# Keys and values as head pairs without tails, states on four 64x64 tiles, and the query cast that moved with them

## The chip, the cores and the metric

One core of one Trainium2 chip. The metric is the device time of one execution in microseconds (us). Engines: PE multiplies matrices, ACT, DVE and POOL (GpSimd) work on vectors, SP issues transfers. Words used below: a "turn" of queries or rows is their transposition on PE, by matmuls with the identity ("the turn to batch 1" is the passage from one batch to the next); the "stream" is the run of a batch's feed-forward matmuls on PE; a "burst" is the matmuls of one batch's state product; the "chain" is the profile's view of the work that ended last, followed back through what each piece waited for.

## The reference, cut to what matters

```python
kv  = einsum('bhsd,bhse->bhde', k, v)      # a 64x64 state for each of 8 heads, 576 rows; 8 batches
out = einsum('bhsd,bhde->bhse', q, kv)
out = out / sqrt(mean(out*out, -1) + 1e-6) * g_norm
x   = out as 4608 rows of 512
xn  = x / sqrt(mean(x*x, -1) + 1e-6) * rms_g
result = (silu(xn @ w_gate) * (xn @ w_val)) @ w_out      # 512 -> 1536 -> 512
```

The feed-forward part is nearly all of the work. The kernel runs it in nine passes (batches 0 to 7 with 512 rows each, then the eight tails of 64 rows as a ninth) and computes the attention of pass n+1 while pass n streams through PE.

## The kernel before

The state product of batches 2 to 7 takes the rows in five chunks of 128; the last chunk holds only the tail's 64 rows, the rest is zero. Batches 0 and 1 (`EARLY`) already have head pairs over 128 partitions.

```python
def kv_pair(ps, b, j, first, last):
    if b < EARLY:                       # 9 chunks, rows 0:64 are one head, 64:128 the other
        for c in range(C):
            for u in range(2):
                rows = slice(u * D, u * D + D)
                PE.matmul(ps[rows, rows], lhsT=pairs_buf(b, "k")[rows, j, c, :], rhs=pairs_buf(b, "v")[rows, j, c, :], ...)
        return
    for t in range(T + 1):              # 5 chunks of 128 rows, one column half for each head
        for u in range(2):
            cols = slice(u * D, u * D + D)
            PE.matmul(ps[cols, cols], lhsT=bufs[b]["k"][:, t, 2 * j + u, :], rhs=bufs[b]["v"][:, t, 2 * j + u, :], ...)

# ... the turn from batch 0 to batch 1 (cut)
att1.kv_products()
for i, engine in enumerate((DVE, SC, DVE, SC)):
    cast_q(1, slice(2 * i, 2 * i + 2), engine)
att1.kv_copy()
# ...
alloc_q(2)
for i in range(2):
    cast_q(2, slice(4 * i, 4 * i + 4), GP)      # batch 2's queries, on POOL
down_part(0, 2, 4)
turns.q_turn(0, SC)                             # first turn of batch 1's queries
# ... F.sums, F.head, F.root: a chain of short DVE instructions, F1y is its last
xs = [F.scale(c, F.outa[c]) for c in range(4)]  # four scalings on DVE, xna
ffn.down_out(0)                                 # output copy on ACT
down_part(1, 8, 12)
f_x(0, xs[0], SC)                               # turn the scaled rows on PE, copy on ACT
f_x(1, xs[1], SC)
ffn.down_out(1)
down_part(2, 8, 12)
f_x(2, xs[2], DVE)                              # needs the bank that f_x(0)'s copy frees
f_x(3, xs[3], DVE)
```

## Time and profile before

| | before |
|---|---|
| time, median of 3 (range) | 320.73 us (320.5 to 321.9) |
| PE busy in a steady batch of 32.7 us | all of it |
| PE idle in the turn from batch 0 to 1 | 0.9 us |
| state product of a steady batch on the chain | 0.75 us |

How to read it: as long as PE has no gap, only matmul time counts. All else counts only in the first 56 us, where PE waits for transfers and then for DVE's short chain, and at one wait near 95 us.

### The profile page before, as it was taken

How to read it: one execution, taken by the hardware profiler on the slowest of the kernel's cores; microseconds unless marked ns; L12 is line 12 of the kernel's file. 1: busy time of each engine (PE TensorE's matmuls, PEld its weight loads, DVE VectorE, ACT ScalarE, POOL GpSimd, SP SyncE). 2: the span in 40 equal slices, each digit the busy share in tenths (PEclk: the TensorE clock that was granted, in tenths of full speed). 3: DMA queues.
4: the chain of work that ended last, by engine and by line, in shares of the span. 5: the costliest groups of instructions: out<-in, count | busy, mean ns of one | idle time of the engine just before them, and what ended most of it. 6: DMA issues, size and time to landing. Idle time of an engine off the chain costs nothing.

```text
span 319.5 us, 5632 instructions
## 1 busy us (share of the span) xinstructions
PE 311.2 (97%) x2179; PEld 151.1 (47%) x2179; DVE 182.2 (57%) x371; ACT 176.1 (55%) x312; POOL 24.8 (8%) x50
## 2 busy tenths in 40 slices
PE   8799998999999999999999999999999999999994
PEld 3485455444444444444444444444444444444443
DVE  4686758679438922893279417951795079504310
ACT  3587456375667466737683767376744374233321
POOL 1274354200000000000000000000000000000000
PEclk9999999999999999999999999999999999999998
DMA  7999999899389657924791389946002600330014
GB/s 263 362 385 387 376 374 293 164 253 241 67 159 312 159 136 189 315 55 113 193 337 48 82 180 229 316 86 197 2 2 60 190 14 1 63 137 0 0 36 99
DMA packets 72903, 54.90 MB, mean 172 GB/s; under 512 B 42280, under 2 KB 64044, under 8 KB 72876
## 3 DMA queue, kind: packets, MB, share of 16 engines
q1 hardware_dynamic: 72496, 53.88, 59.8%
q10 hardware_dynamic: 380, 0.66, 0.6%
q8 instruction: 17, 0.28, 0.4%
q14 instruction: 10, 0.08, 0.1%
HBM read 37.75 MB, written 9.44 MB: 148 GB/s over the span
## 4 chain that ended last, share of the span: by engine, by line
PE 89%; DMA 4%; DVE 2%; SPq 2%; ACT 1%; issue 0%; DVEq 0%
PE g_ps L501 28%; PE v_ps L501 27%; PE o_ps L543 25%; DMA st<-in_v_dram 2%; SPq L319 2%; DMA st<-in_k_dram 1%; PE att_ps L278 1%; PE v_ps L518 1%; PE g_ps L518 1%; DMA qt<-qb 1%; PE att_ps L270 1%; PE g_ps L543 1%; PE v_ps L543 1%; DMA out_dram<-o_sb 1%; DVE xna L482 1%; PE o_ps L518 1%
## 5 line engine op out<-in xcount | busy, mean ns | idle before, releaser
L507 DVE TENSOR_TENSOR h_sb<-silu,v_ps 128x512 bf16<-128x512 bf16 x104 | 71.1, 684 | 98.9 <-ACT silu L506 67.8
L501 PE MATMUL g_ps<-xnt,wg_sb 128*128 128x512 bf16 x416 | 106.9, 379 | 0.0
L501 PE MATMUL v_ps<-xnt,wv_sb 128*128 128x512 bf16 x416 | 106.8, 379 | 0.0
L506 ACT ACTIVATE silu<-g_ps 128x512 bf16<-128x512 f32 x104 | 62.0, 596 | 72.2 <-PE g_ps L501 56.8
L543 PE MATMUL o_ps<-wo_sb,h_sb 128*128 128x512 bf16 x396 | 87.8, 379 | 0.0
L501 PEld LDWEIGHTS <-wv_sb 128*128 128x128 bf16 x416 | 40.7, 98 | 49.1
L543 PEld LDWEIGHTS <-h_sb 128*128 128x128 bf16 x420 | 40.6, 98 | 47.7 <-issue 0.4
L501 PEld LDWEIGHTS <-wg_sb 128*128 128x128 bf16 x416 | 39.6, 98 | 46.4
L106 ACT COPY o_sb<-o_ps 128x512 f32<-128x512 f32 (+1 forms) x34 | 19.7, 579 | 38.1 <-PE o_ps L543 37.3
L106 ACT CAST vb<-st 128x512 bf16<-128x512 f32 (+2 forms) x30 | 17.2, 628 | 4.2 <-DMA st<-in_v_dram 4.2
L397 DVE TENSOR_TENSOR xna<-outa,s1y 128x512 bf16<-128x512 bf16 x28 | 17.9, 683 | 0.0
L380 DVE TENSOR_REDUCE ssq<-sqt 128x16 f32<-128x1024 bf16 x14 | 17.1, 1220 | 0.5
L380 DVE TENSOR_REDUCE ssq<-sq 128x16 f32<-128x1024 bf16 x14 | 17.1, 1219 | 0.5
L106 ACT CAST qb<-st 128x1024 bf16<-128x1024 f32 (+1 forms) x16 | 14.4, 935 | 1.9 <-DMA st<-in_q_dram 1.9
L106 ACT CAST kb<-st 128x512 bf16<-128x512 f32 (+1 forms) x25 | 14.0, 619 | 0.0
L366 ACT ACTIVATE sq<-att_ps 128x512 bf16<-128x512 f32 x14 | 7.6, 594 | 4.3 <-PE att_ps L357 3.6
L643 PE MATMUL att_ps<-kv_all 128*128 128x512 bf16 (+1 forms) x23 | 8.4, 491 | 1.2 <-DVE sel L632 1.2
L379 DVE TENSOR_TENSOR sq<-sq,gsq 128x512 bf16<-128x512 bf16 x14 | 5.9, 422 | 4.9 <-ACT sq L366 4.9
L108 POOL CAST wo_sb<-st 128x512 bf16<-128x512 f32 x12 | 7.3, 633 | 7.4 <-DMA st<-in_moe_w_out_dram 7.4
L108 DVE CAST kb<-st 128x576 bf16<-128x576 f32 (+1 forms) x12 | 5.9, 512 | 3.0 <-DMA st<-in_k_dram 2.9
L366 ACT ACTIVATE sqt<-o_ps 128x512 bf16<-128x512 f32 x14 | 7.6, 598 | 0.0
L371 ACT CAST outa<-att_ps 128x512 bf16<-128x512 f32 x14 | 7.5, 593 | 0.0
(148 smaller groups left out, 185.9 us busy)
## 6 DMA issues: line engine op xcount, KB each, us to landing
out_dram<-o_sb SPq DMA_DIRECT2D x14, 512.0 KB, 3.0
st<-in_q_dram SPq DMA_DIRECT2D x6, 1024.0 KB, 6.5
st<-in_k_dram SPq DMA_DIRECT2D x6, 1024.0 KB, 11.4
st<-in_v_dram SPq DMA_DIRECT2D x6, 1024.0 KB, 12.0
st<-in_moe_w_out_dram SPq DMA_DIRECT2D x6, 512.0 KB, 10.4
st<-in_moe_w_gate_dram SPq DMA_DIRECT2D x4, 512.0 KB, 9.7
st<-in_moe_w_val_dram SPq DMA_DIRECT2D x4, 512.0 KB, 9.2
st<-in_k_dram SPq DMA_DIRECT2D x4, 288.0 KB, 4.3
```

The source lines that it names most:

```text
L106: engine.copy(out=dst, in_=src)
L108: engine.tensor_copy(out=dst, in_=src)
L366: SC.activation(out=self.sq[i][:, :, 0, g:H:2, :], in_=self.banks[i][g], func=ACT.Square)
L371: SC.copy(out=rows[:, :, g:H:2, :], in_=self.banks[i][g])
L380: DVE.reduce_sum(out=self.ssq[:, c], in_=sq, axis=AX.X)
L397: DVE.tensor_tensor(out=self.xna[c], in0=self.outa[c], in1=self.alpha[:, c, :].to_broadcast([128, H, D]), op=OP.mult)
L501: PE.matmul(ps, lhsT=wt[:, s, j * 128 : (j + 1) * 128], rhs=x[:, s, :], start=(s == 0), stop=(s == NS - 1),)
L506: SC.activation(out=silu, in_=g_ps, func=ACT.Silu)
L507: DVE.tensor_tensor(out=self.h[:, j, :], in0=silu, in1=v_ps, op=OP.mult)
L518: PE.matmul(ps[:, u, lo % 256 : lo % 256 + hi - lo], lhsT=wt[:, s, j * 128 : (j + 1) * 128], rhs=xnts[self.n][:, s, lo:hi], start=(s == 0) ...
L543: PE.matmul(self.o_ps[c], lhsT=self.h[:, j, c * 128 : (c + 1) * 128], rhs=wo_sb[:, j, :], start=(j == 0), stop=(j == NF - 1),)
L643: PE.matmul(ps[:, 0:w], lhsT=warm_sb[:, 0:128], rhs=warm_sb[:, 0:w], start=True, stop=True, skip_group_check=True)
```

## The change

Its intent: load every batch's keys and values as pairs of heads over 128 partitions (one transfer of 2304-byte runs instead of a main part and a tail), so that no chunk is half empty, and run the state product on all four 64x64 tiles: even pairs on the two straight tiles, odd pairs on the two crossed ones. The states of odd pairs then lie crossed, and queries, outputs and squares follow. In passing it moves batch 2's query cast from POOL to ACT and DVE, and its state product one unit earlier. The core of the diff:

```diff
-EARLY = 2
 def load_kv(b, name, queue, js=slice(0, NS)):
-    src = srcs[name][b]
-    if b < EARLY: ...                                # paired view
-    queue.dma_start(out=main part, ...)              # 1024-byte runs
-    queue.dma_start(out=tail, ...)                   # 256-byte runs
+    view = srcs[name][b].rearrange("h s d -> (h s d)").rearrange("(j p x) -> p j x", j=NS, p=128)
+    queue.dma_start(out=raws[b, name][:, js, :], in_=view[:, js, :])
 def kv_products(self):
-    self.kv_ps = att_pool.tile([128, NS, 128], FP32, name="att_ps")
-    for j in range(NS):
-        kv_pair(self.kv_ps[:, j, :], self.n, j, j == 0, j == NS - 1)
+    self.kv_ps = [att_pool.tile([128, 2, D], FP32, name="att_ps") for _ in range(2)]
+    for a in range(2):
+        for c in range(C):
+            for x in range(2):
+                for g in range(2):
+                    rows, to = slice(g * D, g * D + D), slice((g ^ x) * D, (g ^ x) * D + D)
+                    PE.matmul(self.kv_ps[x][to, a, :], lhsT=kb[rows, 2 * a + x, c, :], rhs=vb[rows, 2 * a + x, c, :], ...)
 def kv_copy(self):
-    SC.copy(out=kv_all[0:D, n, :, 0:D], in_=ps[0:D, :, 0:D])
-    DVE.tensor_copy(out=kv_all[D:128, n, :, D:128], in_=ps[D:128, :, D:128])
+    for x, engine in enumerate((SC, DVE)):
+        for g in range(2):
+            rows, cols = slice(g * D, g * D + D), slice((g ^ x) * D, (g ^ x) * D + D)
+            cast(engine, kv_all[rows, self.n, x::2, cols], self.kv_ps[x][rows])
 # ... output products, squares, heads: crossed indices, same counts (cut)
-DVE.memset(kv_all[:, 0 : B - 1], 0.0)
+DVE.memset(kv_all[:, 0:2], 0.0)
 # the turn to batch 1
-for i, engine in enumerate((DVE, SC, DVE, SC)):
-    cast_q(1, slice(2 * i, 2 * i + 2), engine)
+for h in (0, 4):
+    cast_heads(1, h, 2, 1, DVE)
+    cast_heads(1, h + 2, 1, 1, SC)
+    cast_heads(1, h + 3, 1, 1, DVE)
 att1.kv_copy()
-alloc_q(2)
-for i in range(2):
-    cast_q(2, slice(4 * i, 4 * i + 4), GP)
 # ...
 ffn.down_out(0)
+alloc_q(2)
+for i in range(T):
+    cast_q(2, i, SC if i < 2 else DVE)
+# ... first two turns of batch 2's queries by transfer (cut)
 down_part(1, 8, 12)
 f_x(0, xs[0], SC)
 # later batches: 4 query casts of 2 heads, 4 + 4 key and value casts; batch 0's odd states crossed by two transfers (cut)
```

More of the change, by code (lines that the diff above doesn't have):

```diff
@@ L90 @@
     kv_all = consts.tile([128, B, NS, 128], BF16, name="kv_all")
-    kbs = [consts.tile([128, T + 1, H, D], BF16, name=f"kb{i}") for i in range(2)]
-    vbs = [consts.tile([128, T + 1, H, D], BF16, name=f"vb{i}") for i in range(2)]
+    kbs = [consts.tile([128, NS, C, D], BF16, name=f"kb{i}") for i in range(2)]
+    vbs = [consts.tile([128, NS, C, D], BF16, name=f"vb{i}") for i in range(2)]
     wg_sb = consts.tile([128, NS, d_ff], BF16, name="wg_sb")
@@ L101, in stage @@
     def stage(n=2048):
-        return stage_pool.tile([128, MAIN * T + MAIN], FP32, name="st")[:, 0:n]
+        return stage_pool.tile([128, NS * C * D], FP32, name="st")[:, 0:n]
     def cast(engine, dst, src):
@@ L116, in alloc_kv, with cast_kv, place @@
     def alloc_kv(b, name):
-        raws[b, name] = stage(MAIN * T + MAIN)
-    def pairs_raw(b, name):
-        return raws[b, name][:, 0 : NS * C * D].rearrange("p (j x) -> p j x", j=NS)
-    def pairs_buf(b, name):
-        flat = bufs[b][name].rearrange("p t h d -> p (t h d)")
-        return flat[:, 0 : NS * C * D].rearrange("p (j c d) -> p j c d", j=NS, c=C)
-    def load_kv(b, name, queue, js=slice(0, NS)):
-        src = srcs[name][b]
-        if b < EARLY:
-            view = src.rearrange("h s d -> (h s d)").rearrange("(j p x) -> p j x", j=NS, p=128)
-            queue.dma_start(out=pairs_raw(b, name)[:, js, :], in_=view[:, js, :])
-            return
-        raw = raws[b, name]
-        queue.dma_start(
-            out=raw[:, 0 : MAIN * T].rearrange("p (h x) -> p h x", h=H),
-            in_=src[:, 0:MAIN, :].rearrange("h (p t) d -> p h (t d)", t=T),
-        )
-        queue.dma_start(
-            out=raw[0:TAIL, MAIN * T :].rearrange("r (h d) -> r h d", h=H),
-            in_=src[:, MAIN:S, :].rearrange("h r d -> r h d"),
-        )
-    KV_CASTS = range(NS + 1)
-    def cast_kv(b, name, i, engine):
-        if b < EARLY:
-            cast(engine, pairs_buf(b, name)[:, i].rearrange("p c d -> p (c d)"), pairs_raw(b, name)[:, i, :])
-        elif i < NS:
-            hs = slice(2 * i, 2 * i + 2)
-            src = raws[b, name][:, 0 : MAIN * T].rearrange("p (h t d) -> p t h d", h=H, t=T)
-            cast(engine, bufs[b][name][:, 0:T, hs, :], src[:, :, hs, :])
-        else:
-            src = raws[b, name][0:TAIL, MAIN * T :].rearrange("r (h d) -> r h d", h=H)
-            cast(engine, bufs[b][name][0:TAIL, T], src)
+        raws[b, name] = stage(NS * C * D).rearrange("p (j x) -> p j x", j=NS)
+    def load_kv(b, name, queue, js=slice(0, NS)):
+        view = srcs[name][b].rearrange("h s d -> (h s d)").rearrange("(j p x) -> p j x", j=NS, p=128)
+        queue.dma_start(out=raws[b, name][:, js, :], in_=view[:, js, :])
+    def cast_kv(b, name, j, engine):
+        cast(engine, bufs[b][name][:, j].rearrange("p c d -> p (c d)"), raws[b, name][:, j, :])
+    def place(h):
+        return h if h % 4 < 2 else h ^ 1
     def load_q(b):
@@ L158, in load_q @@
         raws[b, "q"] = st
-        for hs in (slice(0, 4), slice(4, 8)) if b < EARLY else (slice(0, H),):
+        for hs in (slice(0, 4), slice(4, 8)) if b == 1 else (slice(0, H),):
             nc.sync.dma_start(
@@ L166, in alloc_q, with cast_heads, cast_q @@
         bufs[b]["q"] = qb_pool.tile([128, T, H, D], BF16, name="qb")
-    def cast_q(b, hs, engine):
-        src = raws[b, "q"].rearrange("p (h t d) -> p t h d", h=H, t=T)[:, :, hs, :]
-        cast(engine, bufs[b]["q"][:, :, hs, :], src)
+    def cast_heads(b, h, n, step, engine):
+        src = raws[b, "q"].rearrange("p (h t d) -> p t h d", h=H, t=T)
+        at = place(h)
+        cast(
+            engine, bufs[b]["q"][:, :, at : at + (n - 1) * step + 1 : step, :],
+            src[:, :, h : h + (n - 1) * step + 1 : step, :],
+        )
+    def cast_q(b, i, engine):
+        cast_heads(b, i, 2, 4, engine)
     def load_batch(b):
@@ L263, in alloc_xnt, with kv_pair @@
         xnts[n] = xnt_pool.tile([128, NS, MAIN], BF16, name="xnt")
-    def kv_pair(ps, b, j, first, last):
-        if b < EARLY:
-            for c in range(C):
-                for u in range(2):
-                    rows = slice(u * D, u * D + D)
-                    PE.matmul(
-                        ps[rows, rows], lhsT=pairs_buf(b, "k")[rows, j, c, :], rhs=pairs_buf(b, "v")[rows, j, c, :],
-                        start=(first and c == 0), stop=(last and c == C - 1),
-                    )
-            return
-        for t in range(T + 1):
+    def kv_pair(ps, j):
+        for c in range(C):
             for u in range(2):
-                cols = slice(u * D, u * D + D)
+                rows = slice(u * D, u * D + D)
                 PE.matmul(
-                    ps[cols, cols], lhsT=bufs[b]["k"][:, t, 2 * j + u, :], rhs=bufs[b]["v"][:, t, 2 * j + u, :],
-                    start=(first and t == 0), stop=(last and t == T),
-                )
-    def clear_tail_rows(i, engine):
-        for t in (kbs[i], vbs[i]):
-            engine.memset(t[TAIL:128, T], 0.0)
+                    ps[rows, rows], lhsT=kbs[0][rows, j, c, :], rhs=vbs[0][rows, j, c, :],
+                    start=(c == 0), stop=(c == C - 1),
+                )
     def to_rows(x, n, c, ps, engine):
@@ L306, in kv_products @@
         def kv_products(self):
-            self.kv_ps = att_pool.tile([128, NS, 128], FP32, name="att_ps")
-            for j in range(NS):
-                kv_pair(self.kv_ps[:, j, :], self.n, j, j == 0, j == NS - 1)
+            self.kv_ps = [att_pool.tile([128, 2, D], FP32, name="att_ps") for _ in range(2)]
+            kb, vb = bufs[self.n]["k"], bufs[self.n]["v"]
+            for a in range(2):
+                for c in range(C):
+                    for x in range(2):
+                        for g in range(2):
+                            rows, to = slice(g * D, g * D + D), slice((g ^ x) * D, (g ^ x) * D + D)
+                            PE.matmul(
+                                self.kv_ps[x][to, a, :], lhsT=kb[rows, 2 * a + x, c, :], rhs=vb[rows, 2 * a + x, c, :],
+                                start=(a == 0 and c == 0), stop=(a == 1 and c == C - 1),
+                            )
         def kv_copy(self):
-            n, ps = self.n, self.kv_ps
-            SC.copy(out=kv_all[0:D, n, :, 0:D], in_=ps[0:D, :, 0:D])
-            DVE.tensor_copy(out=kv_all[D:128, n, :, D:128], in_=ps[D:128, :, D:128])
+            for x, engine in enumerate((SC, DVE)):
+                for g in range(2):
+                    rows, cols = slice(g * D, g * D + D), slice((g ^ x) * D, (g ^ x) * D + D)
+                    cast(engine, kv_all[rows, self.n, x::2, cols], self.kv_ps[x][rows])
         def q_rows(self, c):
@@ L322, in q_rows @@
             )
-        def q_turn(self, pair, engine):
-            if pair == 0:
-                self.qt = qt_pool.tile([128, NS, MAIN], BF16, name="qt")
-            ps = att_pool.tile([128, NS, 2, 128], BF16, name="att_ps")
-            for i in range(2):
-                for j in range(NS):
-                    PE.matmul(
-                        ps[:, j, i, :], lhsT=bufs[self.n]["q"][:, 2 * pair + i, 2 * j : 2 * j + 2, :],
-                        rhs=identity, is_transpose=True,
-                        start=(i == 0 and j == 0), stop=(i == 1 and j == NS - 1),
-                    )
-            cast(engine, self.qt[:, :, 256 * pair : 256 * pair + 256], ps.rearrange("p j i t -> p j (i t)"))
         def o_products(self):
@@ L346, in o_products @@
                         rows = slice(g * D, g * D + D)
+                        cols = slice((g ^ j % 2) * D, (g ^ j % 2) * D + D)
                         ps = self.banks[c // 2][g][:, c % 2, j, :]
@@ L352, in o_products @@
                                 PE.matmul(
-                                    ps[us], lhsT=tails_q["t"][rows, c, j, us], rhs=kv_all[rows, 2 * c + u, j, rows],
+                                    ps[us], lhsT=tails_q["t"][rows, c, j, us], rhs=kv_all[rows, 2 * c + u, j, cols],
                                     **flags,
@@ L357, in o_products, with in_place @@
                             PE.matmul(
-                                ps, lhsT=self.qt[rows, j, 128 * c : 128 * c + 128], rhs=kv_all[rows, self.n, j, rows],
+                                ps, lhsT=self.qt[rows, j, 128 * c : 128 * c + 128], rhs=kv_all[rows, self.n, j, cols],
                                 **flags,
                             )
+        def in_place(self, rows, g):
+            fours = rows.rearrange("p c (a h) d -> p (c a) h d", h=4)
+            return fours[:, :, g : 4 - g : 3 - 2 * g, :]
         def put_squares(self, i):
@@ L365, in put_squares @@
             for g in range(2):
-                SC.activation(out=self.sq[i][:, :, 0, g:H:2, :], in_=self.banks[i][g], func=ACT.Square)
+                bank = self.banks[i][g].rearrange("p c (a b) d -> p (c a) b d", b=2)
+                SC.activation(out=self.in_place(self.sq[i][:, 0], g), in_=bank, func=ACT.Square)
         def put_rows(self, i):
@@ L370, in put_rows @@
             for g in range(2):
-                SC.copy(out=rows[:, :, g:H:2, :], in_=self.banks[i][g])
+                bank = self.banks[i][g].rearrange("p c (a b) d -> p (c a) b d", b=2)
+                SC.copy(out=self.in_place(rows, g), in_=bank)
             for c in range(2):
@@ L377, in sums @@
                 self.ssq = stat_pool.tile([128, T, 2, H], FP32, name="ssq")
-            sq = self.sq[c // 2][:, c % 2]
+            sq = self.sq[c // 2][:, :, c % 2]
             DVE.tensor_tensor(out=sq[:, 1], in0=sq[:, 0], in1=gsq8, op=OP.mult)
@@ L430, in turned_tiles @@
                 for g in range(2):
-                    rows = slice(g * D, g * D + D)
+                    rows, cols = slice(g * D, g * D + D), slice((g ^ u) * D, (g ^ u) * D + D)
                     PE.matmul(
-                        banks[g][out], lhsT=kv_all[rows, self.n, 2 * i + u, rows], rhs=self.qt[rows, 2 * i + u, :],
+                        banks[g][out], lhsT=kv_all[rows, self.n, 2 * i + u, cols], rhs=self.qt[rows, 2 * i + u, :],
                         start=True, stop=True,
@@ L678, in state0 @@
         warm(ps, max(dummies, 1), 512 if dummies else 128)
-        kv_pair(ps[:, 0:128], 0, j, True, True)
+        kv_pair(ps[:, 0:128], j)
         return ps
@@ L873 @@
                 round_w(4, "v", s, DVE)
-        if j == 7:
-            clear_tail_rows(0, DVE)
         if j == 8:
@@ L903, in f_heads @@
     def f_heads(j):
-        h = 4 * (j // 2) + j % 2
-        return slice(h, h + 3, 2)
+        h = 4 * (j // 2)
+        return slice(h + 1, h + 3) if j % 2 else slice(h, h + 4, 3)
     def f_o(c):
@@ L925 @@
     att1.kv_products()
-    for i, engine in enumerate((DVE, SC, DVE, SC)):
-        cast_q(1, slice(2 * i, 2 * i + 2), engine)
+    for h in (0, 4):
+        cast_heads(1, h, 2, 1, DVE)
+        cast_heads(1, h + 2, 1, 1, SC)
+        cast_heads(1, h + 3, 1, 1, DVE)
     att1.kv_copy()
-    clear_tail_rows(1, DVE)
     for blk in (1, 2):
@@ L932 @@
             round_wo(blk, i, 1, GP)
-    alloc_q(2)
-    for i in range(2):
-        cast_q(2, slice(4 * i, 4 * i + 4), GP)
     down_part(0, 2, 4)
@@ L961 @@
     ffn.down_out(0)
+    alloc_q(2)
+    for i in range(T):
+        cast_q(2, i, SC if i < 2 else DVE)
+    atts = {b: Att(b) for b in range(2, B + 1)}
+    for c in range(2):
+        atts[2].q_rows(c)
     down_part(1, 8, 12)
@@ L969 @@
     down_part(3, 8, 12)
-    atts = {b: Att(b) for b in range(2, B + 1)}
-    for c in range(T):
+    for c in range(2, 4):
         atts[2].q_rows(c)
@@ L987, in load_q_tails, with cast_q_tails, cross_states @@
         tails_q["b"] = qb_pool.tile([128, T, H, D], BF16, name="qb").rearrange("p t h d -> p t (h d)")
-    def cast_q_tails(c, n, engine):
-        cast(engine, tails_q["b"][:, c : c + n], tails_q["raw"][:, c : c + n])
+    def cast_q_tails(i, engine):
+        dst, src = (tails_q[nm].rearrange("p c (h d) -> p c h d", h=H) for nm in ("b", "raw"))
+        cast(engine, dst[:, :, place(i) : H : 4, :], src[:, :, i:H:4, :])
+    def cross_states():
+        for g in range(2):
+            rows, to = slice(g * D, g * D + D), slice((1 - g) * D, (1 - g) * D + D)
+            nc.sync.dma_start(out=kv_all[to, 0, 1::2, rows], in_=kv_all[rows, 0, 1::2, rows])
     def turn_q_tails(c):
@@ L1007 @@
             steps[0] += [lambda i=i: cast_kv(2, "k", i, DVE) for i in (2, 3)]
-            steps[0] += [lambda: cast_kv(2, "k", NS, GP)]
-            steps[0] += [lambda i=i: cast_kv(2, "v", i, GP) for i in (0, 1, NS)]
-            steps[2] += [lambda i=i: cast_kv(2, "v", i, DVE) for i in (2, 3)]
+            steps[0] += [lambda i=i: cast_kv(2, "v", i, GP) for i in (0, 1)]
+            steps[1] += [lambda i=i: cast_kv(2, "v", i, DVE) for i in (2, 3)]
+        if n == 3:
+            steps[3] += [cross_states]
         if n < B:
             a = atts[n + 1]
-            kv0 = 1 + 2 * int(n == 1)
+            kv0, o0 = (2, 4) if n == 1 else (1, 2)
             if not a.tail:
                 steps[kv0] += [a.kv_products, a.kv_copy]
-            steps[kv0 + 1] += [a.o_products]
+            steps[o0] += [a.o_products]
             for i in range(2):
-                u = kv0 + 1 + 2 * i
+                u = o0 + 2 * i
                 steps[u] += [lambda a=a, i=i: a.put_squares(i)]
@@ L1030 @@
             steps[10] += [lambda b=b: alloc_q(b)]
-            for i in range(2):
-                steps[11] += [lambda b=b, i=i: cast_q(b, slice(4 * i, 4 * i + 4), SC)]
-            for i in KV_CASTS:
-                steps[12 + i // 3] += [lambda b=b, i=i: cast_kv(b, "k", i, SC)]
-                steps[14 + i // 3] += [lambda b=b, i=i: cast_kv(b, "v", i, SC)]
+            for i in range(T):
+                steps[11] += [lambda b=b, i=i: cast_q(b, i, SC)]
+            for i in range(NS):
+                steps[12 + i // 2] += [lambda b=b, i=i: cast_kv(b, "k", i, SC)]
+                steps[14 + i // 2] += [lambda b=b, i=i: cast_kv(b, "v", i, SC)]
             for c in range(T):
@@ L1038 @@
         if b == B:
-            for i in range(2):
-                steps[11] += [lambda i=i: cast_q_tails(2 * i, 2, SC)]
+            for i in range(T):
+                steps[11] += [lambda i=i: cast_q_tails(i, SC)]
             for c in range(T):
```

## The prediction

> **What bounds the kernel now.** I read the page first (engine shares and the chain that ended last), then busy time by stretch, then the chain in order of time around one batch, around the last batch and around batch 1, and then the timeline where the chain leaves TensorE.
>
> ```profile
> span 319.5 us, 5632 instructions
> PE 311.2 (97%) x2179; PEld 151.1 (47%) x2179; DVE 182.2 (57%) x371; ACT 176.1 (55%) x312; POOL 24.8 (8%) x50
> 39.40:56.20 16.80, 15.93 (x198) 9.01 (x197) 12.07 (x28) 10.31 (x18) 8.08 (x13) 1.00 1.08 332
> 154.30:187.00 32.70, 32.70 (x218) 15.24 (x217) 19.09 (x37) 20.81 (x37) 0.00 (x0) 1.00 0.65 169
> ```
>
> Busy PE need not mean a bound PE, but from 56 to 312 us the chain confirms it: it is matmuls end to end. In the fourth line PE is busy for the whole 32.7 us of a batch, ACT for 20.8. In the third (the turn from batch 0 to batch 1) PE idles 0.9 us. So a change pays only by (a) taking matmul time out of the steady batches, or (b) shortening the stretches before 56 us where PE waits. A shorter DMA, a saved cast, a free DVE microsecond buys nothing elsewhere.
>
> The chain at a steady batch's attention part, at the tail batch's, and at batch 1's:
>
> ```profile
> 125.29 0.75 PE att_ps L278 x40
> 126.04 0.97 PE g_ps L501 x4
> ...
> 257.48 0.38 PE att_ps L352 x32
> 257.86 0.29 PE o_ps L352 x32
> 258.15 0.97 PE g_ps L501 x4
> ...
> 41.27 1.25 PE att_ps L270 x72
> ```
>
> L278 is today's state product (128 rows by 64 columns, two tiles of the array in turn), L270 the paired form of batches 0 and 1 on the two diagonal 64x64 tiles, L352 the tail's outputs, the only place that cycles through all four 64x64 tiles. The group after a small-tile burst costs 0.97 where it otherwise costs 0.86, so each burst has a fixed 0.11 at its end; 0.38 against 0.29 for equal halves gives about 0.09 at its start.
>
> **What the Trainium skill says.** "TensorEngine Tiling (Array Packing)", Key Properties: different tiles run weight loads and matmuls in parallel, and changing the tiling mode drains the array. The trace agrees with both: pace per load-and-matmul is (0.75 - 0.09)/40 = 16.5 ns for L278, (1.25 - 0.09)/72 = 16.1 ns for L270, 0.29/32 = 9.1 ns with four tiles; the drain is the 0.09 and 0.11 above. The same page, Gotcha 1, says that row tiles cannot use one PSUM bank simultaneously; the new state products let both row halves write one bank. L270 does that today at the pace of L278, so this trace shows no penalty. "SBUF — State Buffer", Who interferes with whom: a DVE instruction with two SBUF inputs is fully blocked while a GpSimd instruction that reads SBUF runs. The trace shows it in the one place where it matters:
>
> ```profile
> 50.33 0.19 DVE L245 SCALAR_TENSOR_TENSOR F1c<-F1a,Fz 128x32 f32<-128x32 f32 x1
> 50.53 2.02 POOL L108 CAST qb<-st 128x1024 bf16<-128x1024 f32 x2 [1.94 <-DMA st<-in_q_dram]
> 50.56 1.06 DVE L247 SCALAR_TENSOR_TENSOR F1y<-F1c,F0y 128x32 f32<-128x32 f32 x1
> 51.72 3.19 DVE L482 TENSOR_TENSOR xna<-outa,F1y 128x512 bf16<-128x512 bf16 x4
> 53.16 0.40 PE L291 MATMUL att_ps<-identity,xna 128*128 128x128 bf16 x4 [0.67 <-DVE xna L482]
> 53.59 1.19 ACT L106 COPY xnt<-att_ps 128x512 bf16<-128x512 bf16 x2 [1.34 <-PE att_ps L291]
> 53.76 0.40 PE L291 MATMUL att_ps<-identity,xna 128*128 128x128 bf16 x4 [0.21 <-DVE xna L482]
> ```
>
> F1y takes 1.06 us where its sisters take 0.19, and the first scaling of L482 takes 1.379 where the other three take 0.677, both under the POOL cast of batch 2's queries. That is 0.87 + 0.70 = 1.57 us on the only chain that makes PE idle (0.67 + 0.21 us).
>
> **The change part by part.**
>
> State products, batches 2 to 7: 40 matmuls of the 128x64 form become 72 of 64x64. At the four-tile pace of the tail: 72 x 9.1 + 90 = 745 ns, against 750. Work per batch halves in tiles but the count of instructions nearly doubles; it cancels. On the path: 6 x about 0 = 0.0 us.
>
> State products, batch 1: 72 on two tiles become 72 on four: 1.25 - 0.745 = 0.5 us less PE work. What follows decides whether it counts:
>
> ```profile
> 41.94 0.62 ACT L106 CAST qb<-st 128x512 bf16<-128x512 f32 x1 [0.85 <-DMA st<-in_q_dram]
> 41.94 0.43 DVE L108 CAST qb<-st 128x512 bf16<-128x512 f32 x1 [0.90 <-DMA st<-in_q_dram]
> ...
> 42.57 0.37 ACT L313 CAST kv_all<-att_ps 64x256 bf16<-64x256 f32 x1
> 42.90 0.61 PE L856 MATMUL att_ps<-identity,qb 128*128 128x128 bf16 x8
> ```
>
> The first turn of queries (L856) needs the query casts, which start at 41.94 when their transfer lands. In the new kernel DVE casts two heads and then one (0.43 + about 0.29) and is done at 42.68. The states now hold both att_ps buffers, so the turn also needs the first freed by ACT: a one-head cast to about 42.34, then two copies of 64x128. A copy is about 0.25 (0.365 for 256 columns, 0.593 for 512, taken on downwards), so 42.9. PE would be there at about 42.5 and waits to 42.95, against 42.90 now. Gain 0: the saving turns into a wait for the queries and for the buffer.
>
> Query cast of batch 2 from POOL to ACT and DVE: POOL is then idle from 48.6 until batch 2's values land, so F1y ends at 50.75 and the first scaling at 51.48, before PE arrives (about 52.4). PE's 0.88 of idle goes. But ACT now has two casts of 0.62 between the output copy that ends at 52.25 and its copies of the turned rows: these start at 53.5, no earlier than now (53.59). The third turn needs the buffer that the first of them frees, so PE waits to 54.14 and 54.74, does the last turn (0.3) and the last down part (0.86), and starts batch 1's stream at about 55.9 instead of 56.33. Gain 0.45 us.
>
> Batch 2's states move one unit earlier, to about 61 us. Its values land at 58.9 now; single loads with 2304-byte runs in place of 1024 and 256 should bring that to 55 to 57.5. DVE's last value cast ends near 61.1: wait 0 to 0.2 us.
>
> Casts per later batch on ACT: queries 4 x 0.62 instead of 2 x 1.04 (+0.4), keys and values 8 x 0.671 instead of 10 x 0.62 (-0.8). ACT has room; nothing on the path. State copies: four of about 0.25 to 0.29 in place of 0.37 + 0.43; even one after another they end near 127.2, before the output products at 127.80. The smaller clearing of the states at the start (1.55 us now) ends before DVE waits 0.85 us for keys. Output products, squares and sums keep their counts and sizes. The crossing of batch 0's states is two small transfers long before the tail. All 0.
>
> Batch 3's turned queries arrive 0.2 us late today (PEld at 95.3); this may stay or go. Sum: 0.0 + 0.0 - 0.45 + (0 to 0.2) - (0 to 0.2), about -0.5 us.
>
> **The rivals.** (1) The four-tile burst is quicker than the tail's, because the new order goes along diagonals, where successive matmuls share no rows: at 6 ns the burst is 0.52 and six batches give 1.4 us more, 318.8. Against: 9.1 ns is 36 ns per tile, close to the 32 of two tiles, so it looks bound by each tile, not by order. (2) Both row halves writing one bank stall each other: at 16 ns, 72 x 16 + 90 = 1.24 us, 0.5 more in each of six batches, 323.2. For: the skill; against: L270. (3) Batch 2 stalls because values come late or POOL and DVE block each other on casts: 0.5 to 1 us, about 321. (4) The gain of half the load packets shows: no, DMA is hidden once the stream runs (58 to 202 GB/s).
>
> **Range and chances.** 320.73 - 0.5 = 320.2 us. The runs before spread from 320.5 to 321.9, rivals 1 and 3 are the likelier ones and lie within 1.5 us. 319.2 to 321.2 should hold it 8 times in 10. Two per cent is 6.4 us: no rival reaches it either way, so 0.97 for within, the rest split.
>
> **What would show it.** Right: the L278 burst's place on the chain still near 0.75 us with 72 matmuls (rival 1: near 0.5; rival 2: above 1.0); L856 waiting for ACT or the query casts near 42.9; F1y at 0.19 and all four scalings at 0.68; PE waiting near 54 for ACT's copies; the first L501 group at about 55.9; batches still 32.6 apart. Wrong: the steady batches change length by more than 0.1 us each, or PE goes idle in batch 2's first four units.

## More of the kernel before

The page's line on transfers shows how many of them are short; the prediction shows the other lines.

```profile
DMA packets 72903, 54.90 MB, mean 172 GB/s; under 512 B 42280, under 2 KB 64044, under 8 KB 72876
```

## The result, and the profile after

320.25 us median (319.51 to 320.54, 6 runs) against 320.84 (320.5 to 321.9, 6 runs). Ratios here are the mean time of one kernel's fast runs over that of the other's of the same rounds, so not quite the ratio of the quoted medians: 0.9972, interval 0.9953 to 0.9991, which is 0.90 us of 320.84. A repeat on another chip gave 0.997 (0.9954 to 0.9985). Within 2%: same; but the difference is real, since both intervals lie below 1, and the time stamps below put it at about one microsecond.

The page after:

```profile
span 317.5 us, 6031 instructions
PE 309.2 (97%) x2371; PEld 149.9 (47%) x2371; DVE 180.5 (57%) x378; ACT 175.7 (55%) x323; POOL 21.4 (7%) x46
DMA packets 60712, 54.95 MB, mean 173 GB/s; under 512 B 36232, under 2 KB 45708, under 8 KB 60684
```

Twelve thousand packets are gone and the bytes are the same; PE is as full as before. The chain of waits in order of time, first at the turn to batch 1 (start, length, what):

```profile
42.32 0.27 ACT kv_all L104
42.59 0.04 issue
42.63 0.61 PE att_ps L832 x8
...
51.88 0.85 ACT qb L104 x2
52.73 0.19 issue
52.91 1.08 ACT xnt L104 x2
54.00 0.04 issue
54.04 0.38 PE att_ps L262 x4
...
55.29 0.86 PE g_ps L477 x4
```

Then at a steady batch:

```profile
123.88 0.71 PE att_ps L286 x72
124.59 0.97 PE g_ps L477 x4
```

And the timeline of DVE and PE at the same turn (start, length, engine, line, what):

```profile
50.29 0.19 DVE L231 SCALAR_TENSOR_TENSOR F1y<-F1c,F0y 128x32 f32<-128x32 f32 x1
50.59 2.50 DVE L458 TENSOR_TENSOR xna<-outa,F1y 128x512 bf16<-128x512 bf16 x4
52.05 0.61 PE L262 MATMUL att_ps<-identity,xna 128*128 128x128 bf16 x8
53.55 0.87 PE L262 MATMUL att_ps<-identity,xna 128*128 128x128 bf16 x8
```

F1y is back at 0.19 us, the four scalings take 2.50 instead of 3.19, and the DVE wait has left the chain. ACT stands there now: its two query casts hold up its copies of the turned rows (`xnt`), which hold up the third turn. The first query turn (L832) waits for ACT's state copy. Batch 1's state product is off the chain. (The chain view starts a piece where the one before it ended; time stamps are used from here on, and by them the stream starts at 55.12, not 55.29.)

Where the 2.0 us between the two profiled executions lie, from their time stamps:

| stretch | before | after | difference |
|---|---|---|---|
| start to batch 1's state product | 41.20 | 40.86 | -0.34 |
| to the first turn of batch 1's queries | 1.70 | 1.77 | +0.07 |
| first turn to batch 1's stream | 13.27 | 12.49 | -0.78 |
| stream to the start of the last matmul | 258.91 | 258.37 | -0.54 |
| to the end | 4.42 | 4.00 | -0.42 |

The first row is scatter: in the other traces of kernels that differ from the new one only from there on, the same point lies between 40.72 and 41.88, and in the second trace of the kernel before at 43.15. The last row is scatter too (3.97 to 4.45 in all traces, 3.97 to 4.43 among kernels with the new layout). The fourth row is six bursts 0.044 us shorter each (0.626 to 0.582 from first to last matmul start), together 0.26, and a wait of batch 3's output products for turned queries, 0.27. Three differences come back in the second trace of each kernel: the way from batch 1's state product to the stream (0.71 us shorter in this pair, 0.53 in the second), the bursts (0.26), and that wait (0.27 and 0.23). Together 1.0 to 1.2 us; the timing says 0.90 and 0.96, with intervals 0.5 to 0.6 us wide to each side.

### The profile page after: what moved, and what is told of

The parts are those of the page before. It is cut to its first block, busy times and chain, and to the rows that moved or that the text cites. A ratio compares the mean times of both kernels' runs of the same rounds, so it can differ in the third digit from the quotient of the medians.

```text
span 317.5 us, 6031 instructions
## 1 busy us (share of the span) xinstructions
PE 309.2 (97%) x2371; PEld 149.9 (47%) x2371; DVE 180.5 (57%) x378; ACT 175.7 (55%) x323; POOL 21.4 (7%) x46
## 4 chain that ended last, share of the span: by engine, by line
PE 84%; DMA 10%; SPq 3%; ACT 1%; POOL 1%; issue 0%; DVE 0%
PE g_ps L477 27%; PE o_ps L519 26%; PE v_ps L477 26%; DMA st<-in_q_dram 6%; DMA st<-in_moe_w_gate_dram 3%; PE att_ps L286 1%; SPq L199 1%; PE v_ps L519 1%; DMA out_dram<-o_sb 1%; PE att_ps L326 1%; POOL wg_sb L191 1%; SPq L182 1%; SPq L119 1%; PE o_ps L326 0%; PE g_ps L519 0%
## 5 line engine op out<-in xcount | busy, mean ns | idle before, releaser
L104 ACT CAST vb<-st 128x576 bf16<-128x576 f32 x25 | 15.7, 673 | 3.7 <-DMA st<-in_v_dram 3.7
L104 ACT CAST qb<-st 128x512 bf16<-128x512 f32 (+1 forms) x30 | 16.2, 602 | 2.1 <-DMA st<-in_q_dram 2.0
L104 ACT CAST kb<-st 128x576 bf16<-128x576 f32 x20 | 12.5, 673 | 0.0
L619 PE MATMUL att_ps<-kv_all 128*128 128x512 bf16 (+1 forms) x23 | 7.5, 445 | 1.2 <-DVE sel L608 1.2
L106 DVE CAST kb<-st 128x576 bf16<-128x576 f32 x12 | 5.7, 498 | 3.8 <-DMA st<-in_k_dram 3.8
L347 ACT CAST outa<-o_ps 128x512 bf16<-128x512 f32 x14 | 7.5, 591 | 0.0
```

The costliest lines, as they stand in the source:

```text
L104: engine.copy(out=dst, in_=src)
L106: engine.tensor_copy(out=dst, in_=src)
L347: SC.copy(out=self.in_place(rows, g), in_=bank)
L619: PE.matmul(ps[:, 0:w], lhsT=warm_sb[:, 0:128], rhs=warm_sb[:, 0:w], start=True, stop=True, skip_group_check=True)
```

## The experiments

Times are against the kernel before on the same chip. "Stretch" is from the first turn to batch 1's stream.

| run | time, us | before, us | ratio (95%) | stretch, us | burst, ns | batch, us |
|---|---|---|---|---|---|---|
| e1_move_only | 320.16 | 321.22 | 0.9971 (0.9946 to 0.9996) | 12.40 | 626 | 32.62 |
| e2_pool_again | 320.66 | 321.22 | 0.9986 (0.9967 to 1.0006) | 13.11 | 582 | 32.57 |
| e7_late_q | 319.42 | 321.22 | 0.994 (0.992 to 0.996) | 12.05 | 582 | 32.57 |
| e3_two_tiles | 321.1 | 321.22 | 0.999 (0.9969 to 1.001) | 12.49 | 843 | 32.83 |
| e4_pool_reads | 320.65 | 321.0 | 0.9993 (0.9971 to 1.0016) | 13.53 | 582 | 32.57 |
| e8_pool_writes | 320.55 | 321.0 | 0.9983 (0.9964 to 1.0002) | 12.92 | 582 | 32.57 |
| e5_row_order | 320.01 | 321.0 | 0.9976 (0.995 to 1.0003) | 12.49 | 582 | 32.57 |
| e6_bank_by_rows | 319.87 | 321.0 | 0.9965 (0.994 to 0.9989) | 12.49 | 582 | 32.57 |
| e9_straight_only (wrong) | 323.2 | 321.12 | 1.0073 (1.0054 to 1.0092) | 12.49 | 1132 | 33.12 |
| e10_copy_first | 319.48 | 321.12 | 0.9949 (0.9935 to 0.9962) | 13.15 | 582 | 32.57 |
| after_again | 320.09 | 321.12 | 0.997 (0.9954 to 0.9985) | 12.49 | 582 | 32.57 |
| before_again (one look) | 323.35 | 321.12 | none | 13.35 | 626 | 32.62 |

The ratios' intervals are 0.4 to 0.9 us wide to each side; the stretches and bursts repeat to 0.01 to 0.1 us. The first four ran on one chip, the next four on a second, the last four on a third. "Burst" is from the first to the last matmul start and is the usual one of the run; single bursts of e5, e7 and e10 took up to 609 ns.

**e1: the move of the cast alone, on the kernel before.**

```diff
-    alloc_q(2)
-    for i in range(2):
-        cast_q(2, slice(4 * i, 4 * i + 4), GP)
     down_part(0, 2, 4)
 # ...
     ffn.down_out(0)
+    alloc_q(2)
+    for i in range(2):
+        cast_q(2, slice(4 * i, 4 * i + 4), (SC, DVE)[i])
     down_part(1, 8, 12)
```

> The kernel before with one thing changed: batch 2's query cast leaves POOL for ACT and DVE, at the place it has in the new kernel. Theory (the gain at the turn to batch 1 is DVE no longer locked out by POOL): from the first turn of batch 1's queries to the first matmul of batch 1's stream 12.5 us instead of 13.27, F1y at 0.19 us instead of 1.06, all scalings at 0.68; time 0.7 us under the kernel before. Rival (the gain came from the layout, its loads or the four tiles): the stretch stays near 13.2 and the time within 0.2 us of before.

Measured: stretch 12.40, and 0.93 us under the kernel before by the ratio (0.0029 x 321.2), no less than the whole change within the intervals. Timeline of e1:

```profile
50.32 0.19 DVE L247 SCALAR_TENSOR_TENSOR F1y<-F1c,F0y 128x32 f32<-128x32 f32 x1
50.61 2.49 DVE L482 TENSOR_TENSOR xna<-outa,F1y 128x512 bf16<-128x512 bf16 x4
```

The old layout with its old loads shows the new kernel's short chain. The theory holds, the rival falls: neither the loads nor the four tiles are needed for the gain at the turn.

**e2: the cast back on POOL, in the new kernel.**

```diff
     round_wo(blk, i, 1, GP)                    # end of that loop
+    alloc_q(2)
+    for i in range(T):
+        cast_q(2, i, GP)
 # ...
-    alloc_q(2)
-    for i in range(T):
-        cast_q(2, i, SC if i < 2 else DVE)
```

> The new kernel with batch 2's query cast back on POOL at its old place. Theory: F1y or the first scalings are blocked again, together by about 1 to 1.6 us, the stretch from the first turn to the stream is 13.0 to 13.4 us instead of 12.49; the ACT casts no longer stand before the copies of turned rows. Time 0.5 to 0.9 us over the new kernel, so 0 to 0.4 under the kernel before. Rival: stretch and time as in the new kernel.

Measured: stretch 13.11, time between the two kernels, as expected. Timeline of e2:

```profile
50.49 3.20 POOL L106 CAST qb<-st 128x512 bf16<-128x512 f32 x4 [1.91 <-DMA st<-in_q_dram]
50.53 0.61 DVE L231 SCALAR_TENSOR_TENSOR F1y<-F1c,F0y 128x32 f32<-128x32 f32 x1
51.24 3.58 DVE L458 TENSOR_TENSOR xna<-outa,F1y 128x512 bf16<-128x512 bf16 x4
53.27 0.40 PE L262 MATMUL att_ps<-identity,xna 128*128 128x128 bf16 x4 [0.59 <-DVE xna L458]
```

F1y starts just after the first POOL cast and ends with it; with half-size casts it loses 0.42 us instead of 0.87. The four scalings take 3.58 us instead of 2.50, so the two losses come to 1.5 us, and PE waits for DVE again.

**e4 and e8: the sharing by itself.** Both add POOL work that nothing depends on to the new kernel, at the end of POOL's weight casts (the line that allocates the scratch tile is cut).

```diff
+    for i in range(2):
+        cast(GP, scratch, raws[2, "q"][:, 0:1024])      # e4: reads SBUF
```

```diff
+    for i in range(8):
+        GP.memset(scratch, 0.0)                         # e8: only writes SBUF
```

> The new kernel plus two useless POOL casts of 1024 columns of batch 2's queries into a scratch tile, as large and as timed as the two casts of the kernel before; nothing depends on them. Theory (DVE is locked out while POOL reads SBUF): F1y about 1.06 us again and the first scaling about 1.4, the stretch from the first turn to the stream 13.0 to 13.4 us instead of 12.49, time 0.6 to 0.9 us over the new kernel. Rival (only the order of work mattered, not the sharing): F1y 0.19, stretch 12.49, no change.

Measured, e4's timeline:

```profile
50.52 2.48 POOL L107 CAST scratch<-st 128x1024 bf16<-128x1024 f32 x2 [1.83 <-DMA st<-in_q_dram]
50.56 4.18 DVE L459 TENSOR_TENSOR xna<-outa,F1y 128x512 bf16<-128x512 bf16 x4
53.60 0.40 PE L263 MATMUL att_ps<-identity,xna 128*128 128x128 bf16 x4 [1.04 <-DVE xna L459]
```

Stretch 13.53. F1y escaped here (0.19), because the queries landed 0.25 us after its start; the first scalings were hit instead, 4.18 us for four instead of 2.50. Which instruction is hit is chance; the loss is not. The second trace of the kernel before shows the same form: F1y 0.19, four scalings 4.13, stretch 13.35. The time is 0.64 and 0.78 us over e5 and e6, which ran on the same chip and (below) behave as the new kernel: as expected.

> The new kernel plus eight useless POOL clearings of a scratch tile, which write SBUF and read nothing, from about 48.6 us on under the same chain of DVE. Theory (only POOL's reads lock out a DVE instruction with two SBUF inputs): F1y 0.19 us, four scalings 2.5 us in all, stretch 12.49, time as the new kernel. Rival (any POOL work slows DVE): the chain stretches by 0.5 us or more and the stretch grows.

Measured, e8's timeline:

```profile
49.14 0.19 DVE L218 TENSOR_REDUCE Fm<-Ft 128x4 f32<-128x32 f32 x1
49.58 0.43 DVE L237 TENSOR_SCALAR Fyi<-Fz 128x32 int32<-128x32 int32 x1
51.18 0.19 DVE L232 SCALAR_TENSOR_TENSOR F1y<-F1c,F0y 128x32 f32<-128x32 f32 x1
53.89 1.59 DVE L107 CAST qb<-st 128x512 bf16<-128x512 f32 x2
56.19 1.02 PE L478 MATMUL g_ps<-xnt,wg_sb 128*128 128x512 bf16 x3 [0.27 <-DVE xnt L107]
```

Half of the expectation failed. The instructions with two SBUF inputs ran free, as the theory says (F1y 0.19, four scalings 2.50). But some instructions with one SBUF input were held up: Fyi, a tensor_scalar, took 0.43 us instead of 0.18, DVE's two query casts 1.59 instead of 0.76, and those casts pushed DVE's copy of the turned rows into the stream's start, so the stretch was 12.92 and not 12.49 and the time 0.54 and 0.68 us over e5 and e6. Not all were: the reduction Fm, also with one SBUF input, took its usual 0.19 under the same clearings. So POOL's clearings held up another kind of DVE instruction than its casts did in e4.

**e7: the cast later still.** In the new kernel the query casts stand before the copies of the turned rows; here they follow them.

```diff
     ffn.down_out(0)
-    alloc_q(2)
-    for i in range(T):
-        cast_q(2, i, SC if i < 2 else DVE)
     down_part(1, 8, 12)
 # ... f_x(0) to f_x(3)
     down_part(3, 8, 12)
+    alloc_q(2)
+    for i in range(T):
+        cast_q(2, i, SC if i < 2 else DVE)
 # batch 2's query turns by transfer move along with the casts (cut)
```

> The new kernel with batch 2's query cast still on ACT and DVE, but after the copies of the turned rows. Theory (the two ACT casts delay those copies, and the copies hold the two buffers that the third and fourth turn need): PE has no idle between 52 and 55 us, the stretch from the first turn to the stream is 12.05 us instead of 12.49, time 0.4 us under the new kernel. Rival (the buffer is not what PE waits for, or the casts push out the copies of the down products and stall the stream's first units): no change, or 0.3 us slower.

Measured, e7's timeline:

```profile
52.36 0.61 PE L262 MATMUL att_ps<-identity,xna 128*128 128x128 bf16 x8
53.67 0.62 PE L262 MATMUL att_ps<-identity,xna 128*128 128x128 bf16 x8
```

The third and fourth turn now run through in 0.62 us where the new kernel needs 0.87, and end 0.44 us earlier counted from the first two. Stretch 12.05, to the digit of the expectation. Ratio 0.994: this version beats both kernels. Set against the kernel before, it is 0.96 us under the new kernel (0.994 and 0.997 of 321.2, on different chips); e10, the same version with a detail that changed nothing, is 0.61 us under it by medians on one chip. The trace explains 0.44; the rest is within the intervals.

**e3: the same 72 matmuls, two tiles at a time.**

```diff
-                for c in range(C):
-                    for x in range(2):
+                for x in range(2):
+                    for c in range(C):
                         for g in range(2):
```

> The new kernel with the same 72 matmuls of each state product in another order: the two straight tiles for 18 matmuls, then the two crossed ones, so two tiles at a time instead of four. Theory (pace is bound by each tile, about 33 to 36 ns for a load and a matmul): each burst 1.25 us instead of 0.71, six of them on the path, so 3.2 us slower than the new kernel; in batch 1 the longer burst is hidden behind the wait for queries and buffer, the first turn starts within 0.3 us of 42.6. Rival (the pace is bound by issue, 9 ns whatever the tiles): burst 0.71, same time. Second rival (the batch 1 burst is not hidden): first turn 0.5 us later.

Measured: 843 ns from first to last start, not the 1132 that a burst of 1.25 us would have. Neither theory nor rival had it. The trace's single matmul starts, which the merged views do not list, show why: at each of the three switches between the straight and the crossed pair of tiles, the new pair begins while three rounds of the old one are still to run. At the first switch, for instance, a new pair starts 188 ns after the burst's first matmul, and rounds of the old pair still start at about 211, 242 and 274 ns. Which tile a start belongs to is inferred from its place in the 31.7 ns beat. Three switches of three rounds at 31.7 ns are 285 ns, and 1132 - 285 = 847, against 843. So "two tiles at a time" was not what the run did, and the next experiment was needed. The batch 1 part held: the burst is 0.26 us longer and the first turn comes at 42.59.

**e9: straight tiles only.** A run with a wrong result: the odd pairs are put on the straight tiles too.

```diff
-    rows, to = slice(g * D, g * D + D), slice((g ^ x) * D, (g ^ x) * D + D)
+    rows, to = slice(g * D, g * D + D), slice(g * D, g * D + D)
```

> The new kernel with all 72 matmuls of a state product on the two straight tiles (the crossed pairs land in the wrong half, so the result is wrong on purpose). Theory (31.7 ns for each tile's round, so 36 rounds of two tiles): burst 1130 ns from first start to last instead of 582, batches 33.12 us instead of 32.57, six bursts on the path, so 3.3 us over the new kernel and about 2.4 over the kernel before; in batch 1 the longer burst is hidden, the first turn comes 1.7 to 1.8 us after the burst's start, as in all runs so far. Rival (pairing the heads without tails pays by itself): no more than 0.5 us over the new kernel.

Measured, e9's chain at a steady batch:

```profile
125.11 1.25 PE att_ps L286 x72
126.36 0.97 PE g_ps L477 x4
```

Burst 1132 ns, batches 33.12 us, and 3.1 us over the new kernel by medians on the same chip (323.2 against 320.09): paired heads on two tiles would lose 2.1 us against the kernel before. In batch 1 the first turn comes 1.92 us after the burst's start, a little later than expected, since ACT's two state copies follow the longer burst; with bursts of 582 ns it came after 1.57 to 2.03 us in eight traces (e10, whose order differs, left out). That spread is the queries' transfer: counted from the start of the casts of the second half of the queries, which wait for it, the turn comes after 0.88 to 0.89 us in all eight and in e3, and after 1.24 in e9. So 0.35 of the 0.55 us shows there, and the stretch after it is the same 12.49.

**e5 and e6: the order, and the banks.**

```diff
-                    for x in range(2):
-                        for g in range(2):
+                    for g in range(2):
+                        for x in range(2):
```

```diff
-    self.kv_ps[x][to, a, :]
+    self.kv_ps[g][to, a, :]      # and kv_copy to match
```

> The new kernel with the four tiles taken rows in turn (both column tiles of one row half, then of the other) instead of diagonal by diagonal. Theory (each tile takes a new pair every 31.7 ns, whatever the order): 72 matmuls from first start to last in 575 to 600 ns, as the 582 of the new kernel, batches 32.57 us. Rival 1 of the prediction (the diagonal order is what makes the burst shorter than the tail's pace): 640 ns or more, batches 32.63 or more.

> The new kernel with the state's two PSUM buffers split by row half instead of by diagonal, so that the two row halves never write one bank. Theory (no stall from a shared bank): burst 582 ns as in the new kernel, batches 32.57. Rival 2 of the prediction (two row halves in one bank hold each other up): the burst gets shorter, 540 ns or less, batches 32.53 or less.

Measured: 582 ns in both (one burst of e5 596), batches 32.57. The order of the four tiles within a round does not matter (e3 changed the order over many rounds, and there it does), and two row halves that write the two partition halves of one bank do not slow each other. Rivals 1 and 2 of the prediction fall.

**e10: the last wait before the first turn.** e7, and in batch 1 ACT copies the first state bank before its last query cast.

```diff
     for h in (0, 4):
+        if h == 4:
+            att1.kv_copy((0,))
         cast_heads(1, h, 2, 1, DVE)
 # the copy of the other bank stays behind the casts; e7's edit (cut)
```

> The kernel with batch 2's query cast late, and in batch 1 ACT copies the first state bank before its last query cast. Theory (the first turn waits for the buffer that ACT frees after the cast): the wait before the first turn shrinks from 0.26 to about 0.1 us or goes, time 0.1 to 0.25 us under that kernel, 1.6 to 2.0 us under the kernel before. Rival (the queries' transfer alone sets it): no change against that kernel.

Measured: 0.9949, no better than e7. Its timeline:

```profile
42.14 0.27 PE L833 MATMUL att_ps<-identity,qb 128*128 128x128 bf16 x2
43.12 0.73 PE L833 MATMUL att_ps<-identity,qb 128*128 128x128 bf16 x6 [0.70 <-DVE qb L106]
```

The turn starts early and then stands 0.70 us for DVE's query cast, which itself waited for the transfer. (Its stretch of 13.15 counts from that early start.) Where the queries land late, as the rival has it, their transfer sets this point. But it is one trace, and a late one: these casts start 1.90 us after the burst's start, against 0.69 to 1.14 in the traces of e7, the new kernel and the other runs with a 582 ns burst. What the earlier copy is worth when the queries land in time stays open; the times show no gain.

**The two repeats.**

> The new kernel unchanged, on the same chip as the others, and for a second profile. Expected: stretch from first turn to stream 12.49 us, bursts 582 ns, batches 32.57; time 0.9 us under the kernel before. Where batch 1's burst starts (40.7 to 41.9 in the runs so far) is run-to-run scatter.

> The kernel before unchanged, for a second profile. Expected: stretch from first turn to stream 13.27 us, bursts 626 ns, batches 32.62. Open: whether batch 3's output products wait again for turned queries (0.27 us in the first profile); if not, that wait was scatter.

Both as expected. The open point: batch 3's output products waited again in the kernel before (batch 32.85 us instead of 32.62), and in no trace of another kernel, e1 with the old loads among them. So it is hardly scatter, and the old loads alone do not bring it; the query turns by transfer took SP 6.7 us in both traces of the kernel before, 6.02 in e1 and 5.69 in the new kernel. The cast's place alone does not decide it either: e2, the new kernel with the cast back on POOL, had 5.25 and no wait. The cause of this 0.2 to 0.3 us stays open.

## Why the prediction was right

**Time.** 320.2 predicted, 320.25 measured; the sum of the steps was -0.5 us and the measured mean difference -0.90, so the median agrees better than the working deserves: that is luck. The working started from a median of 320.73 for the kernel before, which six runs put at 320.84. What it missed is 0.26 us in the bursts and about 0.3 us at the turn to batch 1, both below.

**State products, batches 2 to 7: "0.0 us".** The mechanism is right, the size a little off. It was 0.71 on the chain instead of 0.745. The tail's 9.1 ns per matmul was the mis-sized term; from first to last start it was 582/72 = 8.1 ns. From the single starts: a tile takes a new load and matmul every 31.7 ns, and the first round takes 52. The old form needs 20 rounds of two tiles: 52 + 18 x 31.7 + 3 = 626 ns, measured 626. e9 needs 36: 52 + 34 x 31.7 + 3 = 1133, measured 1132. The new form needs 18 rounds of four: 52 + 16 x 31.7 + 10 = 569, measured 582, because in its second half the weight loads come 8.3 ns apart, slower than a quarter of 31.7, and one tile falls behind to about 33 ns a round. Seen so, the change saves the empty half of the tail chunk (640 rows become 576, 20 rounds 18), and four tiles are what keeps twice as many half-sized matmuls from costing twice as much: 0.55 us more a batch without them (e9).

**Batch 1's state product: "gain 0".** Right. The burst fell from 1132 to 582 ns and the first turn comes 1.77 us after its start instead of 1.70. It waits 0.46 us for ACT's state copy behind a query cast, as predicted, and that cast waits for the queries' transfer: counted from its start the turn comes after 0.89 us, against 0.96 in the kernel before.

**Query cast off POOL: "gain 0.45 us".** The mechanism is right in each link: F1y 0.19, scalings 0.68 each at their own pace, DVE's wait gone, ACT's copies in its place. The size was 0.78 (second pair of traces: 0.86). The failed term is "these start at 53.5": ACT's casts of 0.62 us were added up end to end, and the two copies after them too (54.14 and 54.74). The casts start 0.52 apart, which the profile before shows too (three casts of 0.62 in 1.66 us). From the output copy to the second copy of turned rows this makes four overlaps of about 0.1 us; counted from the first query turn, the fourth turn of rows came 0.43 us earlier than predicted and the stream 0.34 us. The Trainium skill, "ScalarE: Activation LUTs", What ACT_TABLE_LOAD costs, says that back-to-back ACTIVATEs overlap by about 93 ns; the trace agrees for copies and casts (a cast of 0.616 us and a start 0.524 us after the one before make 1.14 us for two, the length in the trace of the new kernel).

**Batch 2's values, ACT's casts, transfers: "0".** Right in all that the traces show: the values' cast starts at 56.34, no wait at batch 2's products, and 12,000 fewer packets left no gain of their own to find: e1, with the old loads, has the same short stretch. Batch 3's 0.2 us wait "may stay or go"; it went.

## What to carry to other kernels

Where a change bundles a new layout with a small move of work between engines, test the move alone: here moving one cast gave about as much as the whole change (0.93 us), and putting that cast behind the copies that PE waits for took the whole to 1.6 to 1.9 us (e10 and e7). Count array work in rounds per tile before expecting anything from more tiles; four half-sized tiles only pay for the instructions that they double. And before giving a cast to an idle engine, ask whose instructions it will hold up and whose copies it stands in front of.

## What the Trainium skill lacked or had wrong

- "TensorEngine Tiling (Array Packing)", Gotcha 1, says that different row tiles cannot access one PSUM bank at the same time. With two row halves writing different partition halves of one bank, results were right and the burst took 582 ns, the same as with separate banks (e6). By these runs the rule is too broad where the partitions are disjoint.
- The same page gives no pace for a chain of loads and matmuls in one tile. The runs: 31.7 ns for each 64x64 load with 64 columns, first round 52 ns, 8.3 ns between weight loads when four tiles are fed for long.
- "TensorE: Matmul & The Clock Gate", The mechanism, says that matmuls start strictly in program order. In e3, 72 matmuls that change between two pairs of tiles took 843 ns where two tiles in order take 1132, and the starts show the pairs overlapping by three rounds at each change. That they leave program order is inferred from these times, as the trace does not name the tile.
- "SBUF — State Buffer", Who interferes with whom, lacks nothing here: it says that a DVE instruction with two SBUF inputs contends only with POOL's reads, and that casts in a 2-port mode contend with POOL at large. Under POOL reads F1y took 1.06 us instead of 0.19; under POOL clearings F1y 0.19, but DVE's two casts 1.59 instead of 0.76.
